# Top-k attention and a squared-ReLU feed-forward on one core: another order for the eight score products of the last rows, and another planned length for them

## The chip, the cores and the metric

The kernel runs on one core of a Trainium2 chip. The time is that of one execution on the device in microseconds (us); lower is better. Before the change three runs gave 798.44, 799.01 and 802.11 us, median 799.01. Beside them stands one profiled execution, from which all views come.

A core has five instruction streams. TensorE (PE in the profile) multiplies matrices and writes PSUM; the loads of its stationary operand are listed as PEld. VectorE is DVE, ScalarE is ACT, GpSimd is POOL, and SyncE (SP) issues most of the DMAs. They run side by side and wait for each other by semaphores.

## The reference, cut to what matters

The shapes are 8 batches, 8 heads, 576 rows and a head size of 64. Each row of scores keeps its 32 largest entries; then softmax, the product with v, and a feed-forward with squared ReLU (512 to 2048 to 512).

```
scores = scale * np.matmul(q, k.transpose(0, 1, 3, 2))
kth = np.partition(scores, -top_k, axis=-1)[..., -top_k:-top_k + 1]
scores = np.where(scores >= kth, scores, -1000000000.0)
attn = np.exp(scores - np.max(scores, axis=-1, keepdims=True))
attn = attn / (np.sum(attn, axis=-1, keepdims=True) + 1e-09)
x = np.matmul(attn, v)            # then heads side by side: 4608 x 512
g = np.maximum(x @ w_in, 0.0) ** 2
return g @ w_out
```

## The kernel before, in words

**Groups.** Work is cut into 144 groups of two heads by 128 rows. 576 rows are four blocks of 128 and a rest of 64. An ordinary group (gi 0 to 3) is one block of rows of a pair of heads. A last-rows group (gi = Z = 4) takes the 64 left-over rows of two pairs of heads, one pair in PSUM partitions 0 to 63, the other in 64 to 127. There are 128 ordinary groups and 16 of the last rows. In all batches but the last, each two pairs of heads end with a last-rows group; in the last batch both stand first.

**One group, from scores to weights.** TensorE multiplies q with k into three PSUM banks in a row (top_k, lines 638 to 667); there is one such set of three banks in the whole kernel. ScalarE copies the scores to SBUF (tile s, line 669). VectorE folds quarters of the scores on each other, three instructions that read PSUM (fold, line 733), with GpSimd making the complementary halves (line 728), and then extracts the eight largest four times (MAX8 and MATCH_REPLACE8, lines 762 to 774). The next group's scores can be written when the folds and the copy have read the banks. ScalarE then makes a mask from the 32nd value (line 793), TensorE transposes scores and mask into another set of three banks (attend), ScalarE takes the exponential (line 848), and TensorE multiplies with v (collect). The feed-forward runs in between in chunks of rows (feed).

**The score products.** 576 columns for each of two heads don't fit bank borders evenly, so each head's scores are two products: `RUNS` gives head, place, first column and length. Runs 0 and 3 are short (192 columns) and both lie in the middle bank, from head 0 and head 1; runs 1 and 2 are long (384 columns) and have a bank each. Head 0 sits in rows 0 to 63 of TensorE's array and head 1 in rows 64 to 127, so the two can run side by side. Since both short runs write the middle bank from different row halves, run 3 waits for run 0 by a semaphore named `fence`, on which TensorE waits for itself: run 0's last product raises it, and `pe.wait_ge(fence, ...)` stands in front of run 3. Products are in fp32; the profile shows two matmul records for each.

In a last-rows group there are two pairs of heads, and each run is done for pair j = 0 (PSUM partitions 0 to 63) and j = 1 (64 to 127), so eight products with 64 rows each, on four tiles of the array: row half by head, column half by pair. `scores_z` holds their order as a list of (run, pair). The fence is raised by (0, 1) and waited for before (3, 1).

**The order of everything.** The kernel plans its own schedule before it emits instructions. Each operation is entered with `pl.op(engine, duration, priority, function, ...)`, with the tiles that it reads, writes and takes. `Plan.schedule` then plays the program through with these durations, event by event: whenever an engine is free, it takes the ready operation with the lowest priority number whose tiles can be had. What comes out is a fixed order for each engine and a slot for each tile; waits on semaphores follow from that order. The planned duration isn't seen by the chip other than through that order. An ordinary group's score operation is entered with 1.1, a last-rows group's with 1.95.

Of the kernel before, what the change touches and what calls it, by code (L numbers as in the profile page):

```python
# [321 lines left out]
def bass_top_k_attn__then__act_relu_squared_kernel(  # L322
# [31 lines left out]
    LEAD = 40  # L354
# [77 lines left out]
    def tile(nm):  # L432
        return Tile(pools[nm])

    def at(t):
        return mem[t.pool.name][t.slot]
# [7 lines left out]
    def banks(t):  # L444
        b = BASE[t.pool.name]
        return ps32[:, b:b + 3, :].rearrange("p b c -> p (b c)")

    em = Emitter(nc)
    act, vec, gp, pe = nc.scalar, nc.vector, nc.gpsimd, nc.tensor
# [3 lines left out]
    Z = 4  # L453
# [36 lines left out]
    def mm(o, l, r, start, stop=True):  # L490
        return pe.matmul(o, l, r, start=start, stop=stop, skip_group_check=True)  # L491
# [6 lines left out]
    def build(full, weights, pl):  # L498
# [129 lines left out]
        def top_k(gi, qks, tg):  # L628
# [3 lines left out]
            ss, st = Tile(ps_s), tile("s")  # L632
# [17 lines left out]

            def scores_z():
                o = banks(ss)
                for i, j in ((0, 0), (1, 1), (0, 1), (1, 0), (2, 0), (3, 1), (2, 1), (3, 0)):
                    h, to, c0, n_ = RUNS[i]
                    x = at(qks[j])
                    if (i, j) == (3, 1):
                        pe.wait_ge(fence, fences[0])
                    ins = mm(o[64 * j:64 * j + 64, to:to + n_], x[64 * h:64 * h + 64, 512:576],
                             x[64 * h:64 * h + 64, S + c0:S + c0 + n_], i < 3)
                    if (i, j) == (0, 1):  # L660
                        fences[0] += 1
                        ins.then_inc(fence, 1)
                return ins

            qu = sorted(set(qks), key=lambda t: t.num)
            pl.op("pe", 1.1 if gi != Z else 1.95, tg - LEAD, scores if gi != Z else scores_z, r=qu, w=[ss],
                  take=[ss, st], tiled=True)

            cp = [pl.op("act", 1.2, tg - LEAD + 1, lambda: act.copy(  # L669
# [20 lines left out]
            if full:  # L690
                a, sh = tile("a"), tile("sh")
                for rnd in range(4):
                    src = st if rnd == 0 else f
                    for i in range(2):
                        get = dict(r=[st]) if rnd == 0 else dict(hold=[f])
                        if rnd == 3:
# [5 lines left out]
                                       w=[a] if rnd == 0 else [], **(  # L702
                                           get if rnd == 0 else dict(hold=[f, a])))]
# [75 lines left out]
            if not full and n == NGRP - 1:  # L779
                masks = [pl.op("act", .77, tw, lambda: act.activation(  # L780
                    at(wt)[:, 0, :], at(st)[:, 0, 0:S], ACTF.Relu, bias=kth[:, 0, n:n + 1], scale=-1.0),
                    r=[st], w=[wt], take=[wt], after=[ks[0]])]
                masks.append(pl.op("act", .35, tw + .8, lambda: act.activation(
                    at(wt)[:, 1, 0:S % P], at(st)[:, 1, 0:S % P], ACTF.Relu, bias=kth[:, 1, n:n + 1], scale=-1.0),
                    r=[st], w=[wt], after=[ks[1]]))
                masks.append(pl.op("dve", .5, tw - 50, lambda: vec.tensor_scalar(
                    at(wt)[:, 1, S % P:S], at(st)[:, 1, S % P:S], kth[:, 1, n:n + 1], 0.0, ALU.subtract, ALU.min),
                    r=[st], w=[wt], after=[ks[1]]))
                return st, wt, masks
            if not full:  # L790

                for i in range(2):
                    masks[i:] = [pl.op("act", .77, tw + .8 * i, lambda i=i: act.activation(  # L793
                        at(wt)[:, i, :], at(st)[:, i, 0:S], ACTF.Relu, bias=kth[:, i, n:n + 1], scale=-1.0),
                        r=[st], w=[wt], take=[wt] if i == 0 else [], after=[ks[i]])]
                return st, wt, masks

            for i in range(2):
                o = pl.op("gp", .75, tw + 1.3 * i, lambda i=i: gp.tensor_scalar(
                    at(f)[:, i, 0:S], at(st)[:, i, 0:S], kth[:, i, n:n + 1], STEEP, ALU.subtract, ALU.mult),  # L800
                    r=[st], hold=[f], after=[ks[i]])
                pl.op("gp", .75, tw + 1.3 * i + .65, lambda i=i: gp.tensor_scalar(
                    at(wt)[:, i, :], at(f)[:, i, 0:S], BIG, at(sh)[:, i:i + 1], ALU.min, ALU.max),
                    r=[sh], hold=[f], after=[o], w=[wt], take=[wt] if i == 0 else [])
# [245 lines left out]
        def place(b, r0, n_):  # L1050

            for i, c in enumerate(CHUNKS):
                at_ = 0
                for b_, c0, m_ in c:
                    if b == b_ and c0 <= r0 and r0 + n_ <= c0 + m_:
                        return i, at_ + r0 - c0
                    at_ += m_

        for b in range(NB):
# [3 lines left out]
            for hp, gi in seq:  # L1063
                tg = T0 + PER * state["n"]
                hps = (hp, hp if gi != Z else hp + 1)
                for x in hps:
                    if x not in pairs:
                        pairs[x] = load_pair(b, x, tg)
                st, wt, ws_ = top_k(gi, [pairs[x][0] for x in hps], tg)
                if state.get("more"):  # L1070
                    state.pop("more")()
                tt = tg + PER + 2 - TA - TL * max(0, 1 - (NGRP - state["n"]) / NL)
                pt = attend(gi, st, wt, tt, ws_)
                js = [gi] if gi == Z else [g for g in stages if gi in g][0]
                held.setdefault((hp, js[0]), []).append((pt, [pairs[x][1] for x in hps]))
                if gi != js[-1]:
                    continue
                r0, n_ = 128 * js[0], 128 * len(js) if gi != Z else 64
                i, col = place(b, r0, n_)
                first = xts[i] is None  # L1080
                if first:
                    xts[i] = tile("xz" if len(CHUNKS[i]) > 1 else "xt")
                c = CHUNKS[i]
                turned.setdefault(i, []).append(collect(
                    gi, held[hp, js[0]], (xts[i], col, first), hp, tt, last + (c is CHUNKS[-1])))
                left[i] -= n_ * (2 if gi == Z else 1)
                if left[i] == 0:
                    tm = T0 + PER * state["n"] + (NBO if not last else 8)
                    if c is CHUNKS[-1]:
                        feed_last(c, xts[i], tt, turned[i])  # L1090
                        continue
                    feed(c, xts[i], tm, (STEP if b < NB - 2 else 1.9) if not last else 1.5)
# [178 lines left out]
```

## Time and profile before

| | |
|---|---|
| median of three runs | 799.01 us (798.44 to 802.11) |
| profiled execution | 801.75 us, of which the span from first to last instruction is 799.9 us |
| TensorE busy | 89% of the span |
| VectorE busy | 96% |
| ScalarE, GpSimd busy | 88%, 87% |
| granted TensorE clock, mean | 0.975 |
| DMA | 52.65 MB moved, mean 66 GB/s |

How to read the rows. A row of the timeline gives the start in us from the first instruction, the length in us, engine, line, operation, tiles out<-in with the shape, and how many instructions were merged into the row; in brackets stands how long the engine idled before it, and what ended that. Most of TensorE's instructions carry the line of a helper, 491 for products and 494 for transposes, so the tile tells them apart: `ps<-qk` are the score products, with 64*128 (ordinary groups) or 64*64 (last rows) for the stationary operand. A merged row shows the shape of its first product alone. A row of busy time by stretch gives the stretch, its length, and for each engine the busy time and the number of instructions; then the granted clock (1.00 is full), the DMA share and GB/s.

### The profile page before, as it was taken

How to read it: one execution, taken by the hardware profiler on the slowest of the kernel's cores; microseconds unless marked ns; L12 is line 12 of the kernel's file. 1: busy time of each engine (PE TensorE's matmuls, PEld its weight loads, DVE VectorE, ACT ScalarE, POOL GpSimd, SP SyncE). 2: the span in 40 equal slices, each digit the busy share in tenths (PEclk: the TensorE clock that was granted, in tenths of full speed). 3: DMA queues.
4: the chain of work that ended last, by engine and by line, in shares of the span. 5: the costliest groups of instructions: out<-in, count | busy, mean ns of one | idle time of the engine just before them, and what ended most of it. 6: DMA issues, size and time to landing. Idle time of an engine off the chain costs nothing.

```text
span 799.9 us, 27352 instructions
## 1 busy us (share of the span) xinstructions
PE 715.1 (89%) x10420; PEld 525.6 (66%) x10420; DVE 770.2 (96%) x3716; ACT 703.9 (88%) x1058; POOL 698.3 (87%) x643
## 2 busy tenths in 40 slices
PE   7777898979989999988989989998988989989997
PEld 3555666766676766666667667765667766677675
DVE  4989999999999999999999999999999999999995
ACT  3888899989898998989899899988999899897873
POOL 2888999999999899989899888997889989999971
PEclk9988899999999999999999999998999999999999
DMA  8558443122320223031320224204131120100110
GB/s 189 154 144 160 120 125 86 34 51 54 94 53 22 65 51 96 21 82 38 82 62 9 54 61 100 61 22 109 24 97 37 33 53 22 36 8 22 35 36 33
DMA packets 145883, 52.65 MB, mean 66 GB/s; under 512 B 138064, under 2 KB 138064, under 8 KB 145744
## 3 DMA queue, kind: packets, MB, share of 16 engines
q1 hardware_dynamic: 145072, 50.66, 26.2%
q8 instruction: 83, 1.36, 0.7%
q14 instruction: 56, 0.46, 0.2%
q10 hardware_dynamic: 672, 0.16, 0.1%
HBM read 36.70 MB, written 9.44 MB: 58 GB/s over the span
## 4 chain that ended last, share of the span: by engine, by line
DVE 51%; PE 24%; ACT 18%; issue 3%; POOL 3%; DMA 0%; POOLq 0%
PE ps L491 20%; DVE f L771 15%; DVE f L733 11%; DVE c L767 11%; DVE f L762 7%; DVE kth L774 6%; ACT s L669 5%; ACT p L848 4%; PE ps L494 4%; ACT w L793 4%; ACT g L944 2%; POOL u L728 1%; ACT g L959 1%; POOL f L728 1%; ACT qk L621 1%
## 5 line engine op out<-in xcount | busy, mean ns | idle before, releaser
L728 POOL TENSOR_TENSOR f<-u,f 128x864 int32<-128x864 int32 x142 | 265.6, 1870 | 7.7 <-DVE c L767 0.4
L771 DVE MATCH_REPLACE8 f<-c,f 128x98 f32<-128x98 f32 (+2 forms) x864 | 228.4, 271 | 0.0
L793 ACT ACTIVATE w<-s,kth 128x576 bf16<-128x576 f32 x286 | 216.4, 782 | 5.0 <-DVE kth L774 4.6
L491 PE MATMUL ps<-qk 64*128 64x192 f32 (+3 forms) x1280 | 196.9, 446 | 18.2 <-DVE f L733 17.1
L767 DVE MAX8 c<-f 128x8 f32<-128x98 f32 (+2 forms) x864 | 207.5, 274 | 0.0
L728 POOL TENSOR_TENSOR u<-f,s 128x576 int32<-128x576 int32 x142 | 185.5, 1306 | 21.5 <-DVE f L733 21.1
L669 ACT COPY s<-ps 128x1152 f32<-128x1152 f32 x144 | 161.0, 1118 | 36.2 <-PE ps L491 34.8
L848 ACT ACTIVATE p<-ps 128x1152 bf16<-128x1152 f32 x144 | 163.3, 1134 | 25.6 <-PE ps L491 24.8
L491 PEld LDWEIGHTS ps<-qk 64*128 64x128 f32 (+1 forms) x1280 | 134.1, 180 | 55.3 <-DVE f L733 27.9
L491 PE MATMUL ps<-wo,g 128*128 128x512 bf16 (+1 forms) x592 | 141.2, 374 | 3.2 <-ACT g L944 1.1
L491 PE MATMUL ps<-xt,win 128*128 128x256 bf16 (+1 forms) x1152 | 132.9, 264 | 8.3 <-ACT av L895 3.8
L728 POOL TENSOR_TENSOR u<-s 128x288 int32<-128x288 int32 x142 | 113.2, 797 | 30.6 <-ACT s L669 23.7
L494 PEld LDWEIGHTS ps<-ident,s 64*128 64x128 f32 x2592 | 103.2, 141 | 47.3 <-ACT w L793 33.0
L733 DVE TENSOR_TENSOR f<-ps,f 128x288 f32<-128x288 f32 x288 | 127.9, 444 | 0.0
L494 PE MATMUL ps<-ident,s 64*128 64x64 f32 x2592 | 111.4, 229 | 15.7 <-ACT w L793 14.9
L774 DVE MAX8 kth<-f 128x8 f32<-128x296 f32 x288 | 122.9, 457 | 0.0
L762 DVE MAX8 f<-f 128x8 f32<-128x288 f32 x288 | 119.1, 449 | 0.0
L491 PEld LDWEIGHTS ps<-xt,win 128*128 128x128 bf16 x1152 | 95.5, 98 | 32.2 <-ACT av L895 6.7
L491 PEld LDWEIGHTS ps<-wo,g 128*128 128x128 bf16 x592 | 51.4, 98 | 55.1 <-issue 3.7
L944 ACT ACTIVATE g<-ps 128x512 bf16<-128x512 f32 x140 | 81.0, 604 | 2.5 <-PE ps L491 2.3
L491 PE MATMUL ps<-vb,p 128*128 128x65 bf16 (+1 forms) x1600 | 63.0, 196 | 22.2 <-ACT qk L621 5.8
L491 PEld LDWEIGHTS ps<-vb,p 128*128 128x128 bf16 (+1 forms) x1600 | 53.9, 101 | 43.0 <-ACT p L848 9.8
(78 smaller groups left out, 744.5 us busy)
## 6 DMA issues: line engine op xcount, KB each, us to landing
rv<-in_v_dram SPq DMA_DIRECT2D x64, 128.0 KB, 2.4
out_dram<-o SPq DMA_DIRECT2D x32, 256.0 KB, 2.2
rk<-in_k_dram SPq DMA_DIRECT2D x63, 128.0 KB, 2.5
rq<-in_q_dram SPq DMA_DIRECT2D x62, 128.0 KB, 2.5
g<-in_moe_w_in_dram SPq DMA_DIRECT2D x8, 512.0 KB, 4.1
g<-in_moe_w_out_dram SPq DMA_DIRECT2D x8, 512.0 KB, 4.3
xt<-x SPq DMA_TRANSPOSE x70, 2.4
rq<-in_q_dram SPq DMA_DIRECT2D x32, 32.0 KB, 2.5
```

The costliest lines, as they stand in the source:

```text
L491: return pe.matmul(o, l, r, start=start, stop=stop, skip_group_check=True)
L494: return pe.matmul(o, i, ident, is_transpose=True, skip_group_check=True, **kw)
L669: cp = [pl.op("act", 1.2, tg - LEAD + 1, lambda: act.copy(at(st)[:, :, 0:S], two(banks(ss)[:, FIRST_AT:], SECOND, S)), r=[ss], w=[st])]
L728: return pl.op("gp", dur, prio, lambda: gp.tensor_tensor(o().bitcast(I32), x().bitcast(I32), y().bitcast(I32), op), **kw)
L733: return dve(.36, lambda: vec.tensor_tensor(o(), two(banks(ss)[:, FIRST_AT + c:], SECOND, QUART), x(), ALU.max), r=[ss], **kw)
L762: prev[i] = [dve(.065 + HALF / 960, lambda i=i: vec.max(at(f)[:, i, A + 7:A - 1:-1], at(f)[:, i, M + QUART:E]), after=prev[i] + [low], hol ...
L767: lambda i=i, t=t, c0=c0, c1=c1: vec.max(eighth(t, i), at(f)[:, i, c0:c1]),
L771: lambda i=i, t=t, c0=c0, c1=c1: vec.match_replace(at(f)[:, i, c0:c1], eighth(t, i), at(f)[:, i, c0:c1], NEG), hold=[f])]
L774: ks.append(chain(kth, i, prev[i], .065 + (8 + HALF) / 960, lambda i=i: vec.max(eighth(kth, i), at(f)[:, i, A:M + QUART]), hold=[f]))
L793: masks[i:] = [pl.op("act", .77, tw + .8 * i, lambda i=i: act.activation(at(wt)[:, i, :], at(st)[:, i, 0:S], ACTF.Relu, bias=kth[:, i, n:n ...
L848: return act.activation(at(pt)[:, :, :].rearrange("p c (h q) -> p h c q", h=2), bass.AP(x.tensor, x.offset, [x.ap[0], [APART, 2], [64, 9], ...
L944: return act.activation(at(g)[:, 0:kf * nt], bank(hh)[:, 0:kf * nt], ACTF.Relu)
```

## The change

The eight products of a last-rows group are issued in another order: the two short ones of run 0 come first, and of run 2 both stand before the wait on the fence, where one stood after it. Which product raises the fence and which one waits for it stays, and no product, wait or semaphore is added or removed. The planner's duration for the operation goes from 1.95 to 1.2.

```diff
             def scores_z():
                 o = banks(ss)
-                for i, j in ((0, 0), (1, 1), (0, 1), (1, 0), (2, 0), (3, 1), (2, 1), (3, 0)):
+                for i, j in ((0, 0), (0, 1), (1, 1), (1, 0), (2, 0), (2, 1), (3, 1), (3, 0)):
                     h, to, c0, n_ = RUNS[i]
                     x = at(qks[j])
                     if (i, j) == (3, 1):
                         pe.wait_ge(fence, fences[0])
...
-            pl.op("pe", 1.1 if gi != Z else 1.95, tg - LEAD, scores if gi != Z else scores_z, r=qu, w=[ss],
+            pl.op("pe", 1.1 if gi != Z else 1.2, tg - LEAD, scores if gi != Z else scores_z, r=qu, w=[ss],
                   take=[ss, st], tiled=True)
```

## The prediction

> **What bounds the kernel now.** I began with the shares of the engines and the chain that ended last.
>
> ```profile
> PE 715.1 (89%) x10420; PEld 525.6 (66%) x10420; DVE 770.2 (96%) x3716; ACT 703.9 (88%) x1058; POOL 698.3 (87%) x643
> DVE 51%; PE 24%; ACT 18%; issue 3%; POOL 3%; DMA 0%; POOLq 0%
> ```
>
> VectorE works 770.2 of the 799.9 us, and half of the chain is its own. The change touches TensorE alone, so it is worth what VectorE waits for TensorE. Next came busy time by stretch, from the first last-rows group (70 us) to the final groups (780 us). After the stretch stand its length, the busy time of PE, PEld, DVE, ACT and POOL, and the granted clock.
>
> ```profile
> 70.00:100.00 30.00, 25.31 (x355) 19.54 (x351) 28.71 (x140) 27.46 (x42) 26.27 (x23) 0.89 0.64 131
> 100.00:378.00 278.00, 252.64 (x3773) 186.00 (x3772) 277.95 (x1353) 259.93 (x391) 257.43 (x226) 1.00 0.25 62
> 378.00:392.00 14.00, 13.96 (x176) 8.96 (x176) 13.38 (x68) 11.82 (x19) 12.60 (x13) 0.88 0.39 87
> 392.00:463.00 71.00, 65.49 (x982) 47.28 (x978) 70.82 (x344) 63.98 (x95) 63.50 (x56) 1.00 0.21 52
> 463.00:476.00 13.00, 12.55 (x135) 9.23 (x133) 11.89 (x59) 11.26 (x20) 10.97 (x10) 0.87 0.23 52
> 476.00:542.00 66.00, 59.78 (x897) 43.74 (x898) 65.87 (x321) 61.15 (x92) 61.11 (x55) 1.00 0.25 60
> 542.00:566.00 24.00, 21.58 (x314) 16.28 (x309) 22.29 (x107) 20.59 (x35) 17.98 (x16) 0.86 0.35 82
> 566.00:780.00 214.00, 197.55 (x3046) 147.04 (x3040) 213.25 (x1044) 192.47 (x292) 195.74 (x181) 1.00 0.15 37
> ```
>
> Length less VectorE's busy time is its idle time: 1.29, 0.05, 0.62, 0.18, 1.11, 0.13, 1.71 and 0.75, together 5.84 us of 710. That is all that a faster TensorE can give back here. Where the mean clock is below 1, VectorE idles; at full clock hardly. The list of waits names the hand-over, first fold behind ScalarE's copy of the scores, in the window from 64 to 775 us (total, times, longest):
>
> ```profile
> DVE f L733 <- ACT s L669: 5.0, 9, 1.2
> ```
>
> **The change part by part.** First the order. Rows of TensorE's timeline and weight loads: an ordinary score group, then last-rows ones; the last row holds what ran between 100.60 and 100.70 us (count, busy, mean ns).
>
> ```profile
> 89.41 1.24 PE L491 MATMUL ps<-qk 64*128 64x192 f32 x8
> 89.41 0.95 PEld L491 LDWEIGHTS ps<-qk 64*128 64x128 f32 x8
> 70.67 1.80 PE L491 MATMUL ps<-qk 64*64 64x192 f32 x16
> 99.94 0.51 PEld L491 LDWEIGHTS ps<-qk 64*64 64x64 f32 x10
> 100.88 0.20 PEld L491 LDWEIGHTS ps<-qk 64*64 64x64 f32 x6 [0.42 <-PE ps L491]
> 674.32 1.80 PE L491 MATMUL ps<-qk 64*64 64x192 f32 x16
> L491 PE MATMUL ps<-qk 64*64 64x384 f32 x4 | 0.8, 482 | 0.0
> ```
>
> Each product is two matmul records, so the first ten weight loads are five products and the other six are the three behind the fence. Between them the loads idle 0.42 us and resume at 100.88, released by TensorE itself. The last row tells why: at 100.60 only long products (384 columns) are still running. Both short ones into the middle bank are over, and the fence has not reported. As I read it, it reports when the long product issued between them has ended. With the short ones issued first, nothing long stands ahead of the fence. Then (2,0) and (2,1) are also ahead of the wait instead of one of them behind it, and only (3,1) and (3,0) queue on it.
>
> The new length is not in the trace. The eight products lie on four tiles of the array (row half by column half), and each tile gets one short and one long product, two passes each. In the ordinary group each row half gets just that, and the four products take 1.24 us with no idle in their loads. So 1.24 is the floor and 1.80, the fence reporting as late as now, the ceiling. I take 1.25, by the ordinary group, whose fence also hangs on a short product issued first: 0.55 us less. There are 16 such groups (first and last shown), so TensorE gets 16 x 0.55 = 8.8 us. No instruction, DMA or semaphore is added or taken away.
>
> What of it lies on the path? Rows of a group in which VectorE waits, and of one in which it doesn't (start, length, idle before):
>
> ```profile
> 378.04 3.06 PE L491 MATMUL ps<-qk 64*64 64x192 f32 x16 [1.56 <-DVE f L733]
> 381.15 1.12 ACT L669 COPY s<-ps 128x1152 f32<-128x1152 f32 x1 [1.32 <-PE ps L491]
> 382.31 0.46 DVE L733 TENSOR_TENSOR f<-ps,s 128x288 f32<-128x288 f32 x1 [0.44 <-ACT s L669]
> 387.55 0.46 DVE L733 TENSOR_TENSOR f<-ps,s 128x288 f32<-128x288 f32 x1 [0.17 <-ACT s L669]
> 285.05 1.80 PE L491 MATMUL ps<-qk 64*64 64x192 f32 x16
> 287.37 1.11 ACT L669 COPY s<-ps 128x1152 f32<-128x1152 f32 x1
> 288.85 0.44 DVE L733 TENSOR_TENSOR f<-ps,s 128x288 f32<-128x288 f32 x1
> ```
>
> At 285.05 the copy is over at 287.37 + 1.11 = 288.48 and VectorE takes it up at 288.85: 0.37 us of slack, covered by VectorE's own work on the group before. There the 0.55 only makes the slack 0.92. At 378.04 the fold follows the copy at once and VectorE idles 0.44 us, then 0.17 at the next group; a shorter group gives these back. **Term one: -0.61 us.** Without VectorE's cover all 8.8 would be gained.
>
> Second, the planner's 1.95 becomes 1.2. It places operations in order of time, so what it planned ahead of the first last-rows group stays; behind that, all five engines' orders and the tiles' slots may move. TensorE's queue is rewritten (transposes, attention and feed-forward products may change places with the score groups), and with it the loads and transposes on SP, since buffers are planned free earlier. The trace can't show that order. From below its worth is bounded by VectorE's idle time, -5.84; from above by its worst long stretch: from 378 to 566 us it idles 0.62 + 0.18 + 1.11 + 0.13 + 1.71 = 3.75 of 188 us, 2.0%, which over all 710 us is 14.2, or +8.4. I take **0**, the order of now, which lies between, and keep both ends.
>
> Third, the clock. Stretches of 3.41 us on the grid on which the granted clock changes (second number: PE's busy time; the clock stands after POOL's, or after PE's where PE alone is shown):
>
> ```profile
> 347.46:350.88 3.42, 2.02 (x46) 1.61 (x42) 3.42 (x20) 3.42 (x6) 3.32 (x3) 1.00 0.40 120
> 350.88:354.29 3.41, 2.79 (x44) 1.62 (x46) 3.41 (x19) 2.58 (x6) 2.92 (x3) 1.00 0.61 137
> 460.12:463.53 3.41, 2.07 (x44) 1.58 (x44) 3.41 (x14) 3.41 (x7) 2.50 (x4) 1.00 0.45 127
> 463.53:466.94 3.41, 3.41 (x15) 2.46 (x16) 3.20 (x19) 2.43 (x4) 2.93 (x4) 0.50 0.48 106
> 98.28:101.69 3.41, 2.24 (x38) 1.00 0.73 152
> 163.13:166.55 3.42, 2.59 (x40) 1.00 0.11 24
> 286.02:289.43 3.41, 2.49 (x36) 1.00 0.00 0
> ```
>
> The stretch with 2.07 us of TensorE work is followed by half clock, that with 2.02 is not: the border lies near 2.05. The last three hold last-rows groups. Less 0.55 they would have 1.69, 2.04 and 1.94, unless other work moves in, so about two more drops. The price of one: VectorE's idle of 0.62 (378 to 392), 1.11 (463 to 476) and 1.71 (542 to 566, whose clock of 0.86 means 0.14 x 24 / 0.5 = 6.7 us at half, two drops), 3.44 for four, 0.86 each. **Term two: +1.72 us**, between 0 and 3 x 1.11 = 3.3.
>
> The Trainium skill ("TensorE: Matmul & The Clock Gate", Why this matters for your kernels) asks only that idle gaps between bursts stay under about 3 us. The trace differs: 463.53 runs at half clock though the stretch ahead of it was 2.07 us busy. By the page alone term two would be 0 and the time about 1.7 us lower, still no change.
>
> Sum, on the profiled execution of 801.75 us (span 799.9 and 1.85 around it): 801.75 - 0.61 + 1.72 = 802.86. That execution is 2.74 above the median of the runs, 799.01; so **800.1 us**.
>
> **The rivals.** *Faster.* The new order, with TensorE 8.8 us lighter, also removes the other waits of folds for copies: 5.0 us, to 799.0 - 5.0 = 794.0. For it: these waits are behind TensorE and ScalarE, and TensorE is nearly full in each stretch that has them (13.96 of 14.00, 12.55 of 13.00). Against: half clock causes most of them, and shorter groups don't raise the clock; and 278 us without any wait have nothing to give.
>
> *Slower: the plan loses its cushion.* The place is the hand-over from copy to first fold. The planner counted 1.95 for what took 1.80, and now counts 1.2 for what I expect at 1.25, so each last-rows group and what is planned behind it comes 0.2 us later against the plan than before, 3.2 us over 16. The plan packs TensorE's other work into the 0.75 it believes free, of which 0.55 are. Where the slack is 0.37 as at 285.05, one product more ahead of a score group eats it, and VectorE idles. If the waits of 378 to 566 become the rule, it costs the 8.4 worked out above: 807.4. It decides once VectorE's idle time from 70 to 780 us passes 5.84 + 4.0 = 9.8 us. Against it: 1.2 is no farther from 1.25 than the ordinary group's planned 1.1 is from its 1.24.
>
> *Slower: the clock.* If each of the 16 groups brings a drop, 16 x 0.86 = 13.8, or 812. Against: in most places the next products would move in.
>
> *The change doesn't do what it says.* The fence could still report late, so groups stay at 1.80 and the plan is wrong by 0.6 in each: 16 x 0.6 = 9.6 us of TensorE time that the plan lacks, partly under slack of 0.37 a group (5.9), leaving 3.7: 802.7. Against: the ordinary group's loads have no such gap.
>
> **How the numbers follow.** Forecast 0.37, faster 0.22, lost cushion 0.28, clock 0.06, no effect 0.07. The forecast and half of "no effect" lie within 0.5% (795.0 to 803.0), which is about what a measurement of this kernel can tell from no change: same 0.40, slower 0.38 (0.28 + 0.06 + half of 0.07, rounded), faster 0.22. The likeliest case alone ranges from 797.5 to 803. For the whole: the low end is 799.0 - 5.84, about 793.5; the high end is the forecast with the order's +8.4 and a little more of the clock, 809.5.
>
> **What would show it.** Right: last-rows groups of 1.24 to 1.27 us, weight loads twelve and four with no idle on TensorE's own semaphore, VectorE's busy time within 2 us of 770.2, its idle time from 70 to 780 us between 3 and 9 us, two or so more stretches at half clock. Wrong: groups still at 1.80 (the fence), idle time over 9.8 us with folds just behind their copies (the cushion) or under 1.8 us (faster), or an end after 780 us that takes longer than 19.9 us.

## The result and the profile after

Six runs of the changed kernel gave a median of 805.88 us (803.85 to 807.31), six of the kernel before 799.56. The ratio is 1.0074, with a 95% interval of 1.0051 to 1.0096: slower by 0.7%. The profiled execution took 807.31 us, its span 805.4.

The products do what they were to do. The timeline of the changed kernel around a last-rows group, then the first group, the last and the one that took longest:

```profile
280.49 0.85 PEld L491 LDWEIGHTS ps<-qk 64*64 64x64 f32 x16 [0.73 <-DVE f L733]
280.49 1.20 PE L491 MATMUL ps<-qk 64*64 64x192 f32 x16 [0.61 <-DVE f L733]
282.01 1.14 ACT L669 COPY s<-ps 128x1152 f32<-128x1152 f32 x1
284.32 0.46 DVE L733 TENSOR_TENSOR f<-ps,s 128x288 f32<-128x288 f32 x1
...
71.20 1.20 PE L491 MATMUL ps<-qk 64*64 64x192 f32 x16
679.78 1.20 PE L491 MATMUL ps<-qk 64*64 64x192 f32 x16
350.71 1.70 PE L491 MATMUL ps<-qk 64*64 64x192 f32 x16
```

All sixteen weight loads run through without the pause of 0.42 us, and the group takes 1.20 us where it took 1.80. Over all sixteen groups that is 19.7 us of TensorE's time for 31.1. But look at the fold: the copy ends at 282.01 + 1.14 = 283.15, and VectorE takes it up only at 284.32. The 0.37 us of slack of the group at 285.05 before has become 1.17 here. Over all 144 groups the median of this slack went from 0.40 to 0.77 us. The scores are ready earlier, and VectorE is not there.

Where did the time go? VectorE's idle time is no answer. Busy time by stretch in the changed kernel, columns as before:

```profile
70.00:100.00 30.00, 23.05 (x378) 18.62 (x379) 30.00 (x149) 29.13 (x45) 27.72 (x26) 1.00 0.57 136
100.00:378.00 278.00, 249.37 (x3728) 190.17 (x3727) 276.49 (x1335) 256.07 (x385) 256.16 (x224) 0.98 0.26 63
...
463.00:476.00 13.00, 12.08 (x162) 10.23 (x164) 12.93 (x65) 11.03 (x20) 11.07 (x10) 0.87 0.20 43
476.00:542.00 66.00, 59.99 (x893) 43.84 (x885) 65.59 (x316) 60.83 (x92) 60.49 (x54) 1.00 0.27 65
542.00:566.00 24.00, 17.84 (x284) 14.41 (x284) 23.83 (x115) 20.88 (x34) 19.46 (x18) 1.00 0.30 70
566.00:785.50 219.50, 198.69 (x3069) 149.67 (x3066) 216.53 (x1053) 193.76 (x293) 194.91 (x180) 0.98 0.14 36
785.50:805.40 19.90, 15.16 (x225) 11.60 (x224) 10.12 (x35) 8.04 (x16) 3.92 (x4) 1.00 0.10 33
```

I set the last border so that 19.90 us are left behind it, as before; VectorE has as much work in them (10.12 us, 9.93 before). The stretches with long idle times are others. The two sums, VectorE alone, of the kernel before and of the changed one:

```profile
70.00:780.00 710.00, 704.15 (x3427) 0.99 0.24 57
```

```profile
70.00:785.50 715.50, 709.42 (x3428) 0.98 0.23 57
```

The stretch is 5.5 us longer. Idle time is 5.85 us before and 6.08 after; busy time grew by 5.27 us with the same instructions. That the idle time stays hides an exchange: gaps of 0.1 us and more fell from 5.1 to 3.0 us, shorter ones rose from 0.7 to 3.1. Are the instructions slower? No: the page of the changed kernel has them at the same mean or below (MATCH_REPLACE8 270 ns for 271, MAX8 on 288 columns 447 for 449). The first two lines are of the kernel before, the others of the changed one:

```profile
L771 DVE MATCH_REPLACE8 f<-c,f 128x98 f32<-128x98 f32 (+2 forms) x864 | 228.4, 271 | 0.0
L762 DVE MAX8 f<-f 128x8 f32<-128x288 f32 x288 | 119.1, 449 | 0.0
```

```profile
PE 703.0 (87%) x10420; PEld 531.2 (66%) x10420; DVE 775.0 (96%) x3716; ACT 702.9 (87%) x1058; POOL 698.0 (87%) x643
DVE 74%; PE 12%; ACT 9%; issue 3%; POOL 0%; POOLq 0%; DVEq 0%
L771 DVE MATCH_REPLACE8 f<-c,f 128x98 f32<-128x98 f32 (+2 forms) x864 | 227.3, 270 | 0.0
L762 DVE MAX8 f<-f 128x8 f32<-128x288 f32 x288 | 118.7, 447 | 0.0
```

If each is as short and their union is longer, they overlap less. In the timeline most VectorE instructions begin some 80 ns ahead of the end of the one before. Here is a place where they do, a first fold behind the search for the 32nd value (L774) in the kernel before, and one where they don't, in the changed kernel:

```profile
298.23 0.46 DVE L774 MAX8 kth<-f 128x8 f32<-128x296 f32 x1
298.60 0.44 DVE L733 TENSOR_TENSOR f<-ps,s 128x288 f32<-128x288 f32 x1
```

```profile
310.67 0.45 DVE L774 MAX8 kth<-f 128x8 f32<-128x296 f32 x1
311.15 0.46 DVE L733 TENSOR_TENSOR f<-ps,s 128x288 f32<-128x288 f32 x1
```

In the second pair the search ends at 311.12 and the fold begins at 311.15. From start to start it is 485 ns (median over the trace); where nothing holds the fold, as in nine places of the kernel before, it is 376: 109 ns lost. Most of that is overlap, which counts as busy time; the gap of some 35 ns counts as idle. I call such a fold stalled: it begins after a gap under 0.1 us, though its copy ended more than 0.05 us ago. Counted over the traces, 15 of 144 first folds are stalled before and 85 after. The 15 all lie behind 650 us, the 85 all behind 250. 70 x 0.109 = 7.6 us.

The waits for copies, which I had taken for the danger, fell from 5.0 us to 4.0 (window 64 to 775 us), the first row below. TensorE's loads wait longer for folds, over the whole span: the second row is of the kernel before, the third of the changed one.

```profile
DVE f L733 <- ACT s L669: 4.0, 6, 1.3
```

```profile
PEld ps L491 <- DVE f L733: 27.9, 36, 2.2
```

```profile
PEld ps L491 <- DVE f L733: 48.2, 74, 2.2
```

The stalls and the waits for copies together make 7.6 - 1.0 = 6.6 us, against 5.5 by the spans and 6.3 by the medians.

Why is a fold stalled? Tile f has four buffers in turn, so the first fold of group n, entered as writer of its buffer, waits until the search of group n - 4 has ended in it. In the plan of before TensorE is late enough that for most groups this search is long past. With 0.75 us less for the last rows, scores come earlier in the plan, and as first folds have the better priority, each takes its buffer the moment it comes free, as VectorE's very next instruction. The kernel's own lists of waits show it: 15 first folds wait for the instruction just ahead of them in the old plan, 87 in the new. In the new plan these 87 could have begun 0.72 us earlier (median) if their buffer had been free, and all of them begin at the planned end of the search. Both plans end at 789.06 us, so the planner sees no price.

### The profile page after: what moved, and what is told of

Same layout as the page of the kernel before. It is cut to its first block, busy times and chain, and to the rows that moved or that the text cites. A ratio compares the mean times of both kernels' runs of the same rounds, so it can differ in the third digit from the quotient of the medians.

```text
span 805.4 us, 27366 instructions
## 1 busy us (share of the span) xinstructions
PE 703.0 (87%) x10420; PEld 531.2 (66%) x10420; DVE 775.0 (96%) x3716; ACT 702.9 (87%) x1058; POOL 698.0 (87%) x643
## 4 chain that ended last, share of the span: by engine, by line
DVE 74%; PE 12%; ACT 9%; issue 3%; POOL 0%; POOLq 0%; DVEq 0%
DVE f L771 21%; DVE f L733 18%; DVE c L767 16%; DVE f L762 10%; PE ps L491 10%; DVE kth L774 8%; ACT s L669 3%; ACT p L848 2%; PE ps L494 2%; ACT w L793 2%; ACT g L944 2%; ACT g L959 1%; DVE rzall L897 1%; ACT av L895 0%; POOL g L956 0%
## 5 line engine op out<-in xcount | busy, mean ns | idle before, releaser
L767 DVE MAX8 c<-f 128x8 f32<-128x98 f32 (+2 forms) x864 | 210.8, 273 | 0.0
L491 PE MATMUL ps<-qk 64*128 64x192 f32 (+3 forms) x1280 | 186.9, 442 | 27.2 <-DVE f L733 25.9
L848 ACT ACTIVATE p<-ps 128x1152 bf16<-128x1152 f32 x144 | 163.6, 1136 | 19.8 <-PE ps L491 19.2
L494 PEld LDWEIGHTS ps<-ident,s 64*128 64x128 f32 x2592 | 109.4, 143 | 48.7 <-ACT w L793 38.3
L774 DVE MAX8 kth<-f 128x8 f32<-128x296 f32 x288 | 120.2, 455 | 0.0
```

The costliest lines, as they stand in the source:

```text
L494: return pe.matmul(o, i, ident, is_transpose=True, skip_group_check=True, **kw)
L767: lambda i=i, t=t, c0=c0, c1=c1: vec.max(eighth(t, i), at(f)[:, i, c0:c1]),
L774: ks.append(chain(kth, i, prev[i], .065 + (8 + HALF) / 960, lambda i=i: vec.max(eighth(kth, i), at(f)[:, i, A:M + QUART]), hold=[f]))
L848: return act.activation(at(pt)[:, :, :].rearrange("p c (h q) -> p h c q", h=2), bass.AP(x.tensor, x.offset, [x.ap[0], [APART, 2], [64, 9], ...
```

## The experiments

**The order alone, and the length alone**, each on the kernel before.

```diff
-                for i, j in ((0, 0), (1, 1), (0, 1), (1, 0), (2, 0), (3, 1), (2, 1), (3, 0)):
+                for i, j in ((0, 0), (0, 1), (1, 1), (1, 0), (2, 0), (2, 1), (3, 1), (3, 0)):
```

Expected of the first: 

> The new order of the eight products alone, the planned length left at 1.95, so the plan and every engine's order are those of before. Theory (the loss comes from the plan: folds that wait for VectorE's own last instruction): last-rows groups of 1.20 us, 15 stalled folds as before, 798.5 to 800 us, ratio 0.998 to 1.001. Rival (a TensorE with 9 us less work drops its clock more often, and that is the loss): 803 to 806 us, with more stretches at half clock than the 12 of before.

```diff
-            pl.op("pe", 1.1 if gi != Z else 1.95, tg - LEAD, scores if gi != Z else scores_z, r=qu, w=[ss],
+            pl.op("pe", 1.1 if gi != Z else 1.2, tg - LEAD, scores if gi != Z else scores_z, r=qu, w=[ss],
```

Expected of the second: 

> The planned length of 1.2 alone, the old order of the products. Theory: the plan of the changed kernel, some 82 to 87 folds stalled by 0.109 us each; the groups still take 1.80 us, most of it in the slack; 805 to 808 us. Rival (the loss is in the order of the products): 798 to 801 us.

The order alone gave 800.44 us beside 801.93 for the kernel before on this chip, ratio 0.9986 (0.9971 to 1.0002): no change that can be told. Its groups take 1.20 us, 15 folds are stalled, and 12 stretches of 3.41 us are at half clock as before. Over all runs the mean granted clock is 0.976 in the kernel before, with the order alone and in the changed kernel. The length alone gave 809.88, ratio 1.0099 (1.0082 to 1.0117): the loss is in the planned length. That is more than the changed kernel's 1.0074, and above the 805 to 808 us that I expected. The plan now reckons with 1.2 us for groups that take 1.80, and waits for copies rise, while 80 folds are stalled:

```profile
DVE f L733 <- ACT s L669: 7.5, 14, 1.8
```

**The wait taken away, all orders kept.** The first fold writes columns of its buffer that the search does not read, so as a mere user of the buffer it needs no wait; what overwrites the searched columns, the third fold, comes behind the first on VectorE and waits by its own chain.

```diff
-                          hold=[st], w=[f], after=cp, take=[f], late=SLACK if n >= OWN else 0)
+                          hold=[st, f], after=cp, take=[f], late=SLACK if n >= OWN else 0)
```

Expected on the changed kernel: 

> The changed kernel with the first fold entered as a user of its buffer instead of as its writer. Its columns are disjoint from those that the 32nd value's search in the same buffer, four groups ago, still reads, so it need not wait for that search; every engine's order stays that of the changed kernel. Theory: no stalled folds, so 82 x 0.109 = 8.9 us less than 805.9: 797 us, faster than the kernel before. Rivals (waits for ScalarE's copies, the clock, or the order as such cost the time): 804 to 806 us.

It gave 799.37 us, ratio 0.9961 (0.9942 to 0.9981) to the kernel before. By the two ratios that is 0.9961 / 1.0074 = 0.9888 of the changed kernel, 9.0 us less, for 8.9 expected; by the two intervals it is uncertain by some 2.4 us. The 797 us that I had named were reckoned beside 799.56 for the kernel before; here that took 801.93. The same two instructions, in the same order:

```profile
307.08 0.46 DVE L774 MAX8 kth<-f 128x8 f32<-128x296 f32 x1
307.45 0.45 DVE L733 TENSOR_TENSOR f<-ps,s 128x288 f32<-128x288 f32 x1
```

The fold begins 0.37 us behind the search's start, while that still runs. So the loss was this wait, and neither the clock (mean over the runs 0.974, lower than the changed kernel's 0.976) nor TensorE's rewritten queue, which this kernel still has.

**The wait put in, all orders kept.** In the kernel before, the first fold of every group waits also for the instruction one back on VectorE, and in a control for the one two back.

```diff
-            deps = set(o.deps)
+            deps = set(o.deps) | (set(plan.order[e][at[e] - 2:at[e] - 1]) if o.takes and o.takes[0].pool.name == "f" and at[e] > 1 else set())
# the control has at[e] - 3:at[e] - 2, and at[e] > 2
```

One back: 

> The kernel before with a wait for the instruction just ahead on VectorE put on the first fold of every group, where 15 have it already; orders unchanged. It measures the price of one such wait by itself. Theory: up to 128 more folds stalled by 0.109 us, 14 us; less where the fold waits for its copy anyway (some 35 groups start within 0.04 us of the copy's end): 808 to 814 us. Rival (such a wait is free, 376 and 485 ns differ for another reason): 798.5 to 800.5 us.

Two back: 

> The kernel before with a wait on the first fold of every group as in the experiment that cost 1.3%, but for the instruction two back on VectorE instead of the one just ahead; orders unchanged, as many waits. Theory (the price is that the fold can't start while the instruction just ahead is still finishing, 485 - 376 = 109 ns): the instruction two back has ended, so nothing is lost, ratio 0.997 to 1.004. Rival (the wait as an instruction costs, wherever it points): as with the instruction just ahead, 1.011 to 1.015.

One back gave 812.49 us, ratio 1.0128 (1.0109 to 1.0148). The control gave 799.74 beside 801.72, ratio 0.9986 (0.9965 to 1.0007): no cost. It has as many waits, 128 of them for the instruction two back. The first pair of rows is of the kernel that waits for one back, the second of the control:

```profile
308.40 0.30 DVE L771 MATCH_REPLACE8 f<-c,f 128x151 f32<-128x151 f32 x1
308.73 0.46 DVE L733 TENSOR_TENSOR f<-ps,s 128x288 f32<-128x288 f32 x1
```

```profile
300.76 0.30 DVE L771 MATCH_REPLACE8 f<-c,f 128x151 f32<-128x151 f32 x1
300.98 0.45 DVE L733 TENSOR_TENSOR f<-ps,s 128x288 f32<-128x288 f32 x1
```

From start to start 0.33 us and 0.22: 0.11 lost, behind another instruction than the search. 134 folds are stalled, 119 more than before, 13.0 us; waits for copies fell by 1.9 (5.0 to 3.1), so 11.1 are expected and 0.0128 x 801.93 = 10.3 were measured.

**A length between.** The changed kernel with a planned 1.8.

```diff
-            pl.op("pe", 1.1 if gi != Z else 1.2, tg - LEAD, scores if gi != Z else scores_z, r=qu, w=[ss],
+            pl.op("pe", 1.1 if gi != Z else 1.8, tg - LEAD, scores if gi != Z else scores_z, r=qu, w=[ss],
```

> The new order of the products with a planned length of 1.8 instead of 1.2 or 1.95. This plan has 51 first folds that wait for the instruction just ahead of them, between the 15 of the length 1.95 and the 87 of 1.2. Theory (time goes with the number of such folds): 0.9986 + 36 x 0.113 / 800 = 1.004, so 1.002 to 1.006. Rival (the shorter the planned length the worse, by the squeeze on TensorE): a planned 1.8 leaves 0.6 us of cushion over the real 1.2, so as with 1.95: 0.997 to 1.001.

It gave 802.54, ratio 1.001 (0.9996 to 1.0025), outside the theory's 1.002 to 1.006 and at the edge of the rival's 0.997 to 1.001; the interval overlaps both, so this run doesn't decide. Its trace has 52 stalled folds (37 more, 4.0 us) and 4.1 us of waits for copies (0.9 less), which would make 1.004. That trace is of the slowest of the twelve runs, which may be part of the difference.

**The fold freed in the old plan**, once with the new order of the products and once with the old one; the edit is that of the freed fold above.

New order: 

> The new order of the products at the old planned length of 1.95, and the first fold freed of its wait for VectorE. Theory: 15 stalled folds less than with the order alone (ratio 0.9986), 15 x 0.113 = 1.7 us: 0.9965, within 0.995 to 0.999, the same as the changed kernel with the fold freed (0.9961). Rival (the plan of the changed kernel is better by itself once the folds are free): 1 to 2 us slower than that.

Old order: 

> The kernel before, old order and length, with the first fold freed of its wait for VectorE; orders unchanged. It tells what the new order of the products is worth where no fold stalls, beside the new order at the same plan with the fold freed (0.995). Theory: 15 x 0.113 = 1.7 us less than before, ratio 0.998, so 0.3% slower than the one with the new order: a last-rows group is 0.6 us longer, and only where a fold waits for its copy does that cost. Rival (the new order is worth nothing even there): 0.995.

New order: 797.17 us, ratio 0.995 (0.9932 to 0.9967). Old order: 798.64 beside 801.54, ratio 0.9977 (0.9957 to 0.9997). No fold is stalled in either. Both kernels with new order and freed fold are faster than the two kernels compared here; between the two plans, 0.995 and 0.9961 are not told apart. The new order's worth, 0.0027, is as expected, but the two intervals overlap, so it isn't shown. The waits for copies point the same way, new order first; each is of one execution, and both were the fastest of their twelve:

```profile
DVE f L733 <- ACT s L669: 0.4, 2, 0.2
```

```profile
DVE f L733 <- ACT s L669: 3.3, 6, 1.3
```

All kernels together; "expected" is 0.109 us for each stalled fold beyond 15, plus the waits for copies beyond 5.0 us, over 801.7:

```
kernel                          stalled  copy waits  expected  measured
changed kernel                       85      4.0       1.008     1.0074
order alone                          15      4.7       1.000     0.9986
length alone                         80      7.5       1.012     1.0099
changed, fold freed                   0      2.9       0.995     0.9961
before, wait for one back           134      3.1       1.014     1.0128
before, wait for two back            17      4.6       1.000     0.9986
order, length 1.8                    52      4.1       1.004     1.0010
order, length 1.95, fold freed        0      0.4       0.992     0.9950
before, fold freed                    0      3.3       0.996     0.9977
```

The stalled folds and the waits are counted in one execution of each kernel, while "measured" compares medians of runs. Two numbers of the trace carry the table to within 0.003. Three expected values still lie outside the interval of the measured one: the length alone (1.0082 to 1.0117), the length of 1.8 (0.9996 to 1.0025) and the new order with the freed fold (0.9932 to 0.9967). All three expect a larger effect than was measured, and in all three the trace is of the kernel's slowest or fastest execution.

## Why the prediction was right and wrong

The forecast of 800.1 us was 5.8 too low; 805.88 lies in the range, and slower was one of its stronger cases, but not by the mechanism that I gave. The range reached so far up because of the 8.4 us that I allowed the planned length, a bound worked out from idle time; the loss came another way, so that it lies inside is luck.

- *The products.* Right: the fence stood behind a long product. 1.25 us was forecast and 1.20 measured, so the 1.24 of the ordinary group was no floor; why the eight end sooner than the four wasn't tried. 1.20 lies outside the 1.24 to 1.27 that I had named as the sign.
- *Term one, -0.61 us.* The order alone measured 0.9986, -1.1 us, with an interval from -2.3 to +0.2 that holds it. The time that TensorE saves (31.1 us of these groups before, 19.2 with the order alone) was hidden under VectorE, as the slack of 0.37 said.
- *The planned length, taken as 0.* This is the step that failed. I bounded it by VectorE's idle time, -5.84 to +8.4, and took the order of now in between. It cost some 7 us beside the order alone (1.0074 for 0.9986), and not as idle time in sum: the stretch from 70 us has 6.08 us idle for 5.85. The loss sits mostly in busy time, in the overlap of one instruction with the next, 109 ns for each of some 70 more folds that wait for the instruction just ahead. One of the named signs catches it: busy time within 2 us of 770.2 came out as 775.0. The idle time, on which the rivals were to be decided, stayed between 3 and 9.
- *Term two, +1.72 for the clock.* The price holds, the count doesn't. Over the 23 runs of the kernel before beside the order alone, a straight line through time against granted clock gives an estimate of 0.94 us for each 3.41 us at half clock, where I had 0.86. But the mean clock of the runs is the same with the order alone as before. In its profiled execution half clock follows one of the three stretches that I named, with 1.97 us of TensorE's work for the 1.94 that I reckoned. In the other two there are 2.16 and 2.68 us, for 1.69 and 2.04 reckoned: there other work moved in. Other places changed as well, and it is 12 stretches in all, as before. The changed kernel has 13 and the start of one more, in other places. Terms one and two together, +1.1 us, lie outside the -2.3 to +0.2 of the order alone. The longest drop of the changed kernel is this one, where VectorE works 5.95 of 6.83 us:

```profile
607.27:614.10 6.83, 6.22 (x71) 5.31 (x72) 5.95 (x29) 3.14 (x4) 4.75 (x4) 0.50 0.40 89
```

- *The border near 2.05 us of TensorE's work.* It is none. In the changed kernel a stretch with 1.64 us is followed by one at full clock:

```profile
593.62:597.03 3.41, 1.64 (x36) 1.17 (x32) 3.38 (x15) 3.41 (x5) 2.53 (x3) 1.00 0.39 89
597.03:600.44 3.41, 3.36 (x84) 2.95 (x84) 3.41 (x21) 3.21 (x5) 3.22 (x2) 1.00 0.23 84
```

  In the ten traces, from 60 us to 20 us before the end, 101 stretches of this grid that run at full clock have at most 2.07 us of work, and half clock follows 54 of them. It follows none of the 1936 with more. More than 2.07 us of work was enough in every trace here; what decides with less is open.
- *The lost cushion.* Its place, the hand-over from copy to fold, had 5.0 us of waits before and 4.0 after. The rival was right in that the plan does the harm, and its mechanism shows where the plan is really too short: in the length alone the waits rise to 7.5. In the changed kernel the cushion grew (a median of 0.40 to 0.77 over all groups), and the fold was held by VectorE's own queue instead.
- *Faster.* The order alone left 4.7 of the 5.0 us of waits for copies. With the fold freed as well 0.4 were left, in the fastest of the twelve runs of that kernel.

## What to carry to other kernels

A planned duration is an edit to every queue: measure it apart from the code that it describes, by putting each of the two on the kernel alone. When an engine gets busier with the same instructions at the same length, look at the starts, not at the idle time: a wait on the engine's own last instruction hides as lost overlap. Where a buffer's turn makes it, see whether the columns really meet. Giving the planner the price, so that another instruction goes between, is another way, which wasn't tried.

## What the runs showed of the hardware that was not expected

A first fold that waits for the instruction just ahead on VectorE starts about 35 ns after that one's end, where one that isn't held starts mostly 75 to 90 ns ahead of it. From start to start behind the search that is 485 ns for 376: 109 ns. A wait for the instruction two back shows no cost (0.9986, interval 0.9965 to 1.0007, over 128 such waits). The Trainium skill ("VectorE: DVE Perf Modes", The DRAIN you can't avoid) says that a semaphore after each of eight copies cost nothing extra, since the next operation doesn't start until the pipeline is empty, and adds that an operation which isn't held starts earlier. The trace agrees with what it adds: starts overlap ends all through this kernel. It differs on the cost: one wait per group, for the instruction just ahead, made it 1.3% slower (1.0128).
